# The first stage of a fused attention, gating and mixing kernel in another order

## The chip, the cores and the metric

The kernel runs on one core of a Trainium2 chip. The core has a matrix engine (PE), a vector engine (DVE), an engine for activations and copies (ACT), a general engine (POOL), and a queue engine (SP) from which nearly all DMA transfers of this kernel are issued. Each engine runs its own instructions in order, and waits for the others through semaphores. The metric is the device time of one execution in microseconds (us); lower is better.

## The reference, cut to what matters

```python
# attention in chunks of 64 (8 batches, 8 heads, 576 tokens, head width 64)
scores = scale * np.matmul(q_c, k_c.transpose(0, 1, 2, 4, 3))
attn = softmax(scores); x = np.matmul(attn, v_c)          # -> (8, 576, 512)
# gated MLP
h = np.maximum(x @ w_in, 0.0)                             # w_in 512 x 1024
u, v = h[..., :512], h[..., 512:]
v_n = (v - mu) / np.sqrt(var + 1e-06)
v_s = np.einsum('ts,bsd->btd', w_spatial, v_n) + b_spatial[None, :, None]
x = (u * v_s) @ w_out
# token and channel mixer
u = x + (np.maximum(x.T @ w_tok1, 0.0) @ w_tok2).T
out = u + np.maximum(u @ w_ch1, 0.0) @ w_ch2
```

q, k and v are float32. The weights of the gated MLP and of the mixer are float64 and are brought to float32 on the core.

## The kernel before, in words

The program has two halves. In the first, attention and gated MLP run batch by batch, and attention of batch b+1 is woven into the gated MLP of batch b; in the second, the mixer runs over all batches. Matrix products are made in three passes of a high and a low part of each operand (PASSES, line 20). The order of the work is written by hand as three strings of words: FIRST (lines 24 to 36) for batch 0, the conversion of the weights and the attention of batch 1; STEADY for each of the batches 1 to 6; LAST for batch 7 and the way into the second half. `play` (line 1168) calls the function of each word in turn, each engine gets its instructions in that order, and nothing is moved afterwards. So a word early in the string stands early in the queue of every engine that it uses, and a word that waits holds all later words of its engine.

What the words of FIRST stand for (a digit behind a word is a head pair 0 to 3 with 4 for the last 64 tokens, a token block, a column block or a weight piece):

- Attention, with the prefix a for batch 0 and none for batch 1: l, v or L load (SP); in batch 0 x turns q and k on PE and y copies them out (L355, and L349 for the last tokens, ACT); in batch 1 x is transposed on DVE (L377, L378). S scores (PE, L391, L400), s maximum and subtraction (DVE, L410, L411), e exponential (ACT, L417), n row sum and reciprocal (DVE, L421 to L423), z scaling (POOL, L427), T transposes of the probabilities (PE, L435), t their copy (ACT, L443), P times v (PE, L459, L467), p and q high and low part of the result (ACT L478, L488; DVE L480, L492). In batch 1 x4, S4 and so on belong to the last tokens or, for loads and x, to the first pairs of batch 2 (L4, L5, x4).
- Weight pieces 0 to 11: 0 to 3 are the v half of w_in, 4 to 7 its u half by columns, 8 to 11 w_out by columns. wl loads (SP, L130), wa first step (ACT, L144, L145), wm middle (DVE, L153, L155), we end (POOL, L163), wi high part (ACT, L185), wj and wk low part (DVE or POOL, L188).
- Token weights: gl loads them (SP), gt turns one block of columns (PE, L246), gh splits it: a copy on ACT (L83) and a low part on DVE (L84), for the last block, gh4, two copies L256, two small ones L262 and L263 on ACT, and L257 and L264 on DVE.
- Gated MLP: Y is a quarter of the v product of token blocks 0 to 3 (PE, L536), V2 that of the last block (L565); R relu (ACT, L583), r statistics (DVE, L588, L589), F and G add the last block's halves (ACT, L574, L575; DVE, L579), rs and rq give the reciprocal deviation (DVE, L593, L595; ACT, L598, with a load of the activation table), N normalizes (DVE, L602), i and Q high and low part (ACT, L608; DVE, L617), U u product (PE, L625), E relu of it (ACT, L635), W token product (PE, L648), M gate (DVE, L658), H and J its parts (ACT, L661; DVE, L664), A, B and O output product (PE, L674), D its copy and store (ACT, L681; SP, L682).

Several words share storage, and so wait for each other. The products Y, V, U, W, A and O take turns in two buffers of the accumulator memory (`ps_mm`, line 97, two tiles); a new one waits until the one two before has been read. The transposed token weights and P share one bank (tag "p", lines 242 and 449), so a gt waits for p and q of the P before it, and a P waits for the gh before it. Weight pieces 4 to 11 are loaded into two buffers (tag "craw", line 127); attention's q and k take four buffers (tag "raw", line 293), v three (tag "vt", line 359).

Of the kernel before, what the change touches and what calls it, by code (L numbers as in the profile page):

```python
# [10 lines left out]
U32 = mybir.dt.uint32  # L11
# [12 lines left out]
FIRST = """  # L24
al0 wl0 al1 wl1 Z9 ax0 ay0 wa0 aS0 as0 ax1 al2 av0 wl2 wm0 ae0 ay1 an0 we0 az0 aS1 as1 wa1 aT0 wi0 wm1
at0 ax2 al3 av1 wl3 we1 wk0 ae1 ay2 an1 az1 aP0 aS2 ap0 as2 wi1 aq0 aT1 wa2 ae2 at1 ax3 av2 wm2 ay3 an2
az2 aP1 av3 aS3 as3 ap1 ae3 aq1 wj1 ax4 ay4 aT2 we2 wa3 wi2 at2 an3 wm3 az3 gl0 gl1 gl2 wl4 wl5 aP2 aS4
as4 ap2 wk2 we3 aq2 Y0 ae4 aT3 at3 wi3 an4 wk3 az4 Y1 aP3 L0 ap3 aq3 wa4 aT4 at4 Y2 aP4 wm4 ap4 aq4 Y3
x0 we4 wl6 wa5 L1 gt0 wi4 R0 R1 gh0 wm5 r0 S0 V2 s0 wk4 R3 we5 gt1 wi5 F r1 e0 R2 r3 wa6 G r2 gh1 wk5
U0 wl7 n0 x1 R4 z0 wm6 gt2 r4 we6 rs rq gh2 wi6 S1 U1 E0 wk6 s1 N0 T0 gt3 wa7 i0 Q0 t0 e1 gh3 N1 U2  # L30
wm7 n1 N2 we7 gt4 i1 wi7 E1 z1 Q1 gh4 wk7 i2 N3 N4 L2 wl8 U3 i4 Q2 x2 P0 p0 L3 S2 i3 E2 Q3 T1 q0 Q4
W0 t1 E3 s2 wl9 wa8 wm8 wa9 W1 we8 x3 e2 M0 M1 wi8
wm9 S3 W2 n2 wl10 we9 H0 wa10 W3 M2 s3 H2 wi9 J0 wl11 M3 z2 P1 S4 wk8 H1 J1 wj9 p1 q1 J2 H3
e3 wm10 T2 J3 A0 s4 n3 we10 A1 wa11 t2 L4 z3 wi10 B0 wm11 D0 e4 B1 P2 p2 D1 we11 T3 wj10 O2 n4
q2 t3 x4 z4 L5 P3 T4 wi11 p3 q3 D2 wk11 t4 O3 P4 D3 p4 q4
"""
STEADY = """
x1 ca L2 S0 V0 s0 e0 ca n0 z0 cm ce V1 cm S1 R1 r1 R0 r0 ce T0 R2 r2 R3 r3 t0 V2 U0 s1 e1
# [17 lines left out]
def attention_gmlp_mixer(  # L56
# [17 lines left out]
    DM = 512  # L74
# [1108 lines left out]
    pieces = by_rows(w_in, w_in_t, DM) + by_cols(w_in, w_in_t) + by_cols(w_out, w_out_t)  # L1183

    def load_piece(i):
        if i < 4:

            if i % 2 == 0:
                pieces[i].raw = pieces[i + 1].raw = lp.tile(
                    [128, 2, DM, 2], U32, tag=f"g{i // 2}", bufs=1, name="wv_raw")  # L1190
            pieces[i].load(pieces[i].raw[:, i % 2])
        else:
            pieces[i].load()

    class Stream:
# [19 lines left out]
    play(FIRST, {  # L1215
        **attn[0].ops("a"), **attn[1].ops(), **Gate(0).ops(), "Z": warm,
        "wl": load_piece, "wa": lambda i: pieces[i].start(), "wm": lambda i: pieces[i].mid(),
        "we": lambda i: pieces[i].end(), "wi": lambda i: pieces[i].to_hi(),
        "wj": lambda i: pieces[i].to_lo(nc.vector), "wk": lambda i: pieces[i].to_lo(nc.gpsimd),
# [34 lines left out]
    c1, s1 = {}, {}  # L1254
# [70 lines left out]
    for b in range(NB):  # L1325
        for n in range(21):
            g, i = divmod(n, 7)
# [9 lines left out]
    for n in range(7 * NB):  # L1337
        b, i = divmod(n, 7)
# [53 lines left out]
```

## Time and profile before

| what | value |
|---|---|
| timed runs, median (3 runs) | 1242.53 us (1241.91 to 1242.74) |
| the profiled execution | 1244.85 us |
| its span, first to last instruction | 1242.3 us |
| PE busy | 1192.9 us, 96% of the span |
| weight loads of PE busy | 1127.6 us, 91% |
| DVE busy | 879.5 us, 71% |
| ACT busy | 501.0 us, 40% |
| POOL busy | 161.7 us, 13% |
| mean granted PE clock | 0.984 of full |
| DMA, mean over the span | 158 GB/s |

A row of the timeline gives the start in us from the span's start, the time that it takes, the engine, the line of the kernel, the operation, output and input tiles, shapes and count; in brackets the idle time of the engine before it and the engine and line that ended it. A row of the waits gives who waited for whom, the total in us, how often, and the longest. A row of the windows gives a stretch, its length, the busy time of each engine with its count of instructions, the granted clock of PE, the share of the DMA engines and GB/s. Times of a group of equal instructions run from the first start to the last end. Busy shares say little here, because the program has stages with different limits; the first stage, up to about 118 us, is what the change touches.

### The profile page before, as it was taken

The numbers are of one execution on the slowest core, as the hardware profiler recorded it, in microseconds if no ns is written. First come the engines' busy times: TensorE is split into PE (matmuls) and PEld (weight loads), VectorE is DVE, ScalarE is ACT, GpSimd is POOL, SyncE is SP. The second block draws the span as 40 slices with busy tenths as digits, with TensorE's granted clock in tenths as the row PEclk, the third lists the DMA queues.
The fourth block names the chain that finished last, engine by engine and source line by source line (L and its number), as shares of the span: only waits on it lengthen the run. The fifth ranks groups of instructions, "written<-read, shape, count | busy, mean of one in ns | idle before, by whom it ended". The sixth has DMA issues, their size and how long they took to land. (4 is left out here: it accounts for less than half of the span.)

```text
span 1242.3 us, 25079 instructions
## 1 busy us (share of the span) xinstructions
PE 1192.9 (96%) x10042; PEld 1127.6 (91%) x10042; DVE 879.5 (71%) x1365; ACT 501.0 (40%) x797; POOL 161.7 (13%) x156
## 2 busy tenths in 40 slices
PE   6889999999999999998899999999998999999997
PEld 5779898989898989997889999999998999999997
DVE  5667757576766767366776776776768887787786
ACT  5464535354545444434332232332225434334431
POOL 2323111111121121013400000000005100000000
PEclk8889999999999999999989999999999999999999
DMA  9735537484838381178445565565385576666773
GB/s 228 150 77 127 96 104 134 100 172 107 200 85 206 89 213 38 56 158 203 140 142 170 170 189 172 163 187 166 134 303 190 195 217 199 183 188 189 214 213 45
DMA packets 405704, 196.00 MB, mean 158 GB/s; under 512 B 348434, under 2 KB 368338, under 8 KB 405588
## 3 DMA queue, kind: packets, MB, share of 16 engines
q1 hardware_dynamic: 400724, 193.81, 58.9%
q8 instruction: 79, 1.29, 0.5%
q10 hardware_dynamic: 4864, 0.59, 0.3%
q14 instruction: 37, 0.30, 0.1%
HBM read 123.16 MB, written 71.17 MB: 156 GB/s over the span
## 5 line engine op out<-in xcount | busy, mean ns | idle before, releaser
L1010 PE MATMUL ps_c<-ub,wt 128*128 128x288 f32 x2016 | 288.9, 298 | 6.6 <-ACT s L1042 2.5
L1010 PEld LDWEIGHTS ps_c<-ub,wt 128*128 128x128 f32 x2016 | 278.2, 190 | 12.9 <-ACT s L1042 3.8
L1010 PE MATMUL ps_c<-hb,wt 128*128 128x288 f32 x2016 | 268.9, 295 | 1.6 <-DVE hb L1099 1.6
L1010 PEld LDWEIGHTS ps_c<-hb,wt 128*128 128x128 f32 x2016 | 268.2, 188 | 2.2 <-DVE hb L1099 2.2
L625 PE MATMUL ps_u<-xt,w_in 128*128 128x288 f32 x768 | 110.3, 304 | 7.7 <-ACT ut L635 3.3
L625 PEld LDWEIGHTS ps_u<-xt,w_in 128*128 128x128 f32 x768 | 107.3, 195 | 9.1 <-ACT ut L635 3.5
L1098 ACT CAST hb<-h 128x1728 fp32r<-128x1728 f32 x40 | 64.8, 1638 | 122.7 <-DVE h L1091 50.0
L648 PE MATMUL ps_s<-ws,vn 128*128 128x288 f32 x768 | 108.5, 297 | 2.8 <-ACT ut L635 2.8
L648 PEld LDWEIGHTS ps_s<-ws,vn 128*128 128x128 f32 x768 | 103.5, 188 | 4.7 <-ACT ut L635 4.4
L674 PE MATMUL ps_o<-g,w_out 128*128 128x288 f32 x768 | 106.6, 296 | 0.0
L674 PEld LDWEIGHTS ps_o<-g,w_out 128*128 128x128 f32 x768 | 102.5, 188 | 1.0 <-ACT h L899 0.2
L1099 DVE TENSOR_TENSOR hb<-h,hb 128x1728 fp32r<-128x1728 f32 x40 | 78.2, 1955 | 28.6 <-ACT hb L1098 28.6
L536 PE MATMUL ps_v<-w_in,xt 128*128 128x512 f32 x384 | 92.7, 399 | 0.0
L536 PEld LDWEIGHTS ps_v<-w_in,xt 128*128 128x128 f32 x384 | 72.1, 190 | 16.7
L427 POOL TENSOR_TENSOR e<-e,sm 128x512 f32<-128x512 f32 (+1 forms) x40 | 39.1, 976 | 236.6 <-DVE sm L423 194.3
L163 POOL TENSOR_TENSOR ctmp<-ctmp,craw 128x512 uint32<-128x512 uint32 (+3 forms) x41 | 49.6, 1211 | 135.4 <-DVE ctmp L155 64.6
L926 PE MATMUL ps_u<-w,h 128*128 128x288 f32 x384 | 62.2, 299 | 4.4 <-DVE xh L931 4.4
L967 ACT CAST ub<-xh 128x576 fp32r<-128x576 f32 x56 | 37.4, 672 | 70.0 <-DVE xh L974 66.8
L926 PEld LDWEIGHTS ps_u<-w,h 128*128 128x128 f32 x384 | 54.8, 190 | 5.7 <-DVE xh L931 5.5
L968 DVE TENSOR_TENSOR ub<-xh,ub 128x576 fp32r<-128x576 f32 x56 | 43.0, 770 | 21.1 <-ACT ub L967 20.6
L868 ACT CAST xn<-nat 128x512 fp32r<-128x512 f32 x40 | 24.8, 619 | 76.8 <-DVE nat L866 75.6
L887 PE MATMUL ps_h<-xn,w 128*128 128x512 f32 x192 | 51.8, 403 | 3.4 <-ACT xn L868 3.3
(148 smaller groups left out, 1609.5 us busy)
## 6 DMA issues: line engine op xcount, KB each, us to landing
hd<-c SPq DMA_DIRECT2D x120, 288.0 KB, 2.2
h<-hd SPq DMA_DIRECT2D x40, 864.0 KB, 6.9
craw<-in_moe_w_ch_dram SPq DMA_DIRECT2D x24, 512.0 KB, 4.9
x_raw<-x2d SPq DMA_DIRECT2D x160, 64.0 KB, 2.7
xh<-x2d SPq DMA_DIRECT2D x16, 576.0 KB, 6.0
u2d<-xh SPq DMA_DIRECT2D x16, 576.0 KB, 3.1
u<-u2d SPq DMA_DIRECT2D x16, 576.0 KB, 6.8
x2d<-x2o SPq DMA_DIRECT2D x31, 288.0 KB, 2.9
```

The lines of the kernel that those rows point to most:

```text
L163: nc.gpsimd.tensor_tensor(out=tu, in0=tu, in1=raw[:, :, 0], op=ALU.add)
L427: nc.gpsimd.tensor_tensor(out=e, in0=e, in1=sm.to_broadcast([128, e.shape[1], 64]), op=ALU.mult)
L536: nc.tensor.matmul(ps, lhsT=self.xt[kc][:, p, 128 * ti:128 * ti + 128], rhs=w_in_t[r][:, kc, DM:2 * DM], start=kc == 0 and n == 0, stop=kc ...
L625: nc.tensor.matmul(ps[:, h, 0:HALF], lhsT=w_in_t[r][:, kc, 128 * m:128 * m + 128], rhs=self.xt[kc][:, p, HALF * h:HALF * h + HALF], start= ...
L648: nc.tensor.matmul(ps[:, h, 0:HALF], lhsT=lhsT, rhs=rhs[:, HALF * h:HALF * h + HALF], start=n == 0, stop=n == len(ops) - 1)
L674: nc.tensor.matmul(ps[:, h, 0:HALF], lhsT=w_out_t[r][:, kc, 128 * m:128 * m + 128], rhs=self.g[p][:, kc, h], start=kc == 0 and n == 0, sto ...
L887: nc.tensor.matmul(ps[kk], lhsT=PB["w1"][r][:, m, ksl], rhs=xn[:, p], start=m == 0 and n == 0, stop=False)
L926: nc.tensor.matmul(ps, lhsT=h1[:, kk, p, 128 * m:128 * m + 128], rhs=PB["w2"][r][:, kk, HALF * h:HALF * h + HALF], start=n == 0, stop=n == 5)
L968: eng.tensor_tensor(out=lo, in0=x, in1=f32(hi), op=ALU.subtract)
L1010: nc.tensor.matmul(ps, lhsT=lhsT, rhs=rhs, start=first and n == 0, stop=n == len(ops) - 1, skip_group_check=True)
L1098: nc.scalar.copy(out=hi, in_=x)
L1099: nc.vector.tensor_tensor(out=lo, in0=x, in1=f32(hi), op=ALU.subtract)
```

## The change

Only FIRST and the loading of two weight pieces change. The string's first two lines and half of its third stay; the rest is written in another order:

```diff
-az2 aP1 av3 aS3 as3 ap1 ae3 aq1 wj1 ax4 ay4 aT2 we2 wa3 wi2 at2 an3 wm3 az3 gl0 gl1 gl2 wl4 wl5 aP2 aS4
...
+az2 aP1 av3 aS3 as3 ap1 aq1 wj1 ae3 aT2 at2 ax4 ay4 we2 an3 wa3 wi2 az3 wm3 gl0 gl1 gl2 wl4 wl5 wl6 wl7
...
     def load_piece(i):
-        if i < 4:
+        if i < 4 or 6 <= i < 8:
 
             if i % 2 == 0:
                 pieces[i].raw = pieces[i + 1].raw = lp.tile(
-                    [128, 2, DM, 2], U32, tag=f"g{i // 2}", bufs=1, name="wv_raw")
+                    [128, 2, DM, 2], U32, tag=f"g{i // 2 % 3}", bufs=1, name="wv_raw")
             pieces[i].load(pieces[i].raw[:, i % 2])
```

Pieces 6 and 7, the second half of w_in's u half, are loaded into the buffer that held pieces 0 and 1 (tag "g0"), not into the two buffers of pieces 4 and 5, and stand on SP's queue directly behind these, ahead of the attention loads L0 and L1 of batch 1. The token weights are turned between the head pairs of batch 0 and the Y products: gt0 ahead of Y0, gt1 behind Y1, gt2 behind Y3, gt3 behind U0, gt4 behind U1, and P0 of batch 1 directly behind gt4. The four relus R0, R1, R3, R2 follow each other. The string has one line less, so that each later line has a number lower by one than in the kernel before; the rows below carry each kernel's own numbers.

The first place is ACT behind the exponential of head pair 3 of batch 0. `last` are the copies y of the last tokens, `wv_raw` and `w_in` belong to weight pieces 3 and 2, and `aT` is the copy at2. Before:

```order
L417 ACTIVATE e<-e 128x512
L349 COPY last_167<-ps_x 128x256
L349 COPY last_168<-ps_x 128x256
L144 ACTIVATE ctmp<-wv_raw 128x512
L145 ACTIVATE wv_raw<-wv_raw 128x512
L185 CAST w_in_84<-ctmp 128x512
L443 COPY aT<-ps_t 128x512
```

and after the change:

```order
L416 ACTIVATE e<-e 128x512
L442 COPY aT<-ps_t 128x512
L348 COPY last_167<-ps_x 128x256
L348 COPY last_168<-ps_x 128x256
L143 ACTIVATE ctmp<-wv_raw 128x512
L144 ACTIVATE wv_raw<-wv_raw 128x512
L184 CAST w_in_84<-ctmp 128x512
```

The copy at2 has moved ahead of five instructions.

The second place is ACT from the exponential e1 of batch 1 to the high part of weight piece 7 (the last `w_in` row in both). `ws_r` are the parts of gh4, `vn` and `vr` high parts i of the normalized v, `ut` the relus E. Before:

```order
L417 ACTIVATE e<-e 128x512
L83 CAST ws_88<-ps_w 128x576
L608 CAST vn_92<-v_163 128x512
L185 CAST w_in_84<-ctmp 128x4x128
L635 ACTIVATE ut<-ps_u 128x576
L256 CAST ws_r_90<-ps_w 64x576 x2
L262 CAST ws_r_91<-ws_rows 1x576
L263 CAST ws_r_91<-ws_rows 1x576
L608 CAST vn_92<-v_164 128x512
```

and after the change, in two pieces, up to gh4 and from there to piece 7:

```order
L416 ACTIVATE e<-e 128x512
L184 CAST w_in_84<-ctmp 128x4x128
L634 ACTIVATE ut<-ps_u 128x576
L143 ACTIVATE ctmp<-wv_raw 128x512
L144 ACTIVATE wv_raw<-wv_raw 128x512
L607 CAST vn_92<-v_164 128x512
L255 CAST ws_r_90<-ps_w 64x576 x2
```

and from gh4's one-row copies on to piece 7:

```order
L261 CAST ws_r_91<-ws_rows 1x576
L262 CAST ws_r_91<-ws_rows 1x576
L607 CAST vn_92<-v_165 128x512
L477 CAST xt<-ps_p 128x512
L634 ACTIVATE ut<-ps_u 128x576
L607 CAST vr_94<-v_166 128x512
L609 CAST vr_95<-v_166 64x512
L184 CAST w_in_84<-ctmp 128x4x128
```

Before, piece 7's high part stood ahead of gh4; now it stands seven rows behind it, and piece 6's (the first `w_in` row) and both first steps of piece 7 stand between e1 and gh4.

The third place is ACT at the end of the stage, around the high part of the last weight piece (the last `w_out` row), the parts p4 (`xt`, four copies) and the output copies D (`x2o`). Before:

```order
L443 COPY aT<-ps_t 128x512
L185 CAST w_out_86<-ctmp 128x4x128
L478 CAST xt<-ps_p 128x512
L681 COPY x2o<-ps_o 128x576
L443 COPY aT<-ps_t 128x256
L681 COPY x2o<-ps_o 128x576
L488 CAST xt<-ps_p 128x64 x4
```

and after the change:

```order
L680 COPY x2o<-ps_o 128x576 x2
L442 COPY aT<-ps_t 128x256
L487 CAST xt<-ps_p 128x64 x4
L184 CAST w_out_86<-ctmp 128x4x128
L680 COPY x2o<-ps_o 128x576 x2
```

The last weight piece's high part now stands behind p4, no longer ahead of p3.

More of the change, by code (lines that the diff above doesn't have):

```diff
@@ L26 @@
 at0 ax2 al3 av1 wl3 we1 wk0 ae1 ay2 an1 az1 aP0 aS2 ap0 as2 wi1 aq0 aT1 wa2 ae2 at1 ax3 av2 wm2 ay3 an2
-az2 aP1 av3 aS3 as3 ap1 ae3 aq1 wj1 ax4 ay4 aT2 we2 wa3 wi2 at2 an3 wm3 az3 gl0 gl1 gl2 wl4 wl5 aP2 aS4
[L28 to L35, printed above, removed]
+az2 aP1 av3 aS3 as3 ap1 aq1 wj1 ae3 aT2 at2 ax4 ay4 we2 an3 wa3 wi2 az3 wm3 gl0 gl1 gl2 wl4 wl5 wl6 wl7
+aP2 aS4 as4 ap2 aq2 wk2 ae4 aT3 at3 we3 an4 wi3 gt0 wk3 az4 Y0 gh0 wa4 L0 aP3 ap3 aq3 wm4 Y1 gt1 we4 wa5
+aT4 at4 gh1 wm5 wi4 Y2 x0 aP4 ap4 aq4 we5 wk4 L1 Y3 gt2 R0 R1 R3 R2 r0 wi5 S0 gh2 r1 V2 F r2 r3 s0 wk5
+G R4 e0 U0 r4 rs rq x1 n0 z0 wa6 gt3 N0 gh3 i0 E0 wm6 S1 T0 t0 U1 Q0 N1 we6 i1 s1 gt4 e1 wi6 E1 Q1 N2 wa7
+i2 gh4 wk6 P0 n1 wm7 L2 wl8 U2 Q2 N3 i3 z1 we7 p0 E2 N4 i4 wi7 Q3 q0 x2 wk7 T1 t1 U3 S2 Q4 s2 E3 W0 P1
+e2 p1 q1 L3 wl9 n2 wa8 wm8 z2 W1 we8 x3 M0 wi8 wa9 wm9 T2 t2 S3 W2 s3 M1 H0 wl10 we9 e3 n3 J0 z3 P2 p2
+W3 M2 H1 wi9 wa10 q2 J1 wk8 S4 wl11 H2 M3 wm10 T3 t3 s4 J2 H3 e4 we10 wj9 J3 A0 P3 p3 n4 wa11 A1 wi10 q3
+L4 z4 B0 wm11 D0 B1 D1 T4 t4 we11 wj10 O2 P4 p4 wi11 q4 D2 wk11 x4 L5 O3 D3
 """
```

## The prediction, on record before the changed kernel was run

> **What bounds the kernel now.** I read the page first, then the core's windows cut where the first stage changes character, then what the matrix engine (PE) waited for between 28 and 119 us, then the granted clock in slices of one microsecond, then the timeline row by row.
>
> ```profile
> span 1242.3 us, 25079 instructions
> ```
> ```profile
> 0.00:28.10 28.10, 19.04 (x253) 15.93 (x253) 15.06 (x27) 13.66 (x24) 8.38 (x13) 0.88 0.98 213
> 28.10:47.70 19.60, 16.05 (x152) 12.89 (x153) 10.28 (x25) 10.27 (x24) 8.33 (x8) 0.91 0.65 171
> 47.70:85.20 37.50, 28.53 (x266) 25.29 (x264) 26.74 (x53) 21.95 (x38) 10.90 (x9) 0.82 0.59 97
> 85.20:118.40 33.20, 33.20 (x378) 31.96 (x380) 25.18 (x47) 16.54 (x31) 11.10 (x9) 1.00 0.53 117
> ```
> ```profile
> PE ps_p L459 <- ACT aT L443: 3.6, 1, 3.6
> PE ps_u L625 <- ACT ut L635: 3.3, 1, 3.3
> PE ps_u L625 <- ACT v L583: 3.2, 1, 3.2
> PE ps_u L625 <- POOL w_in L188: 1.2, 1, 1.2
> ```
> ```profile
> 56.00:57.00 1.00, 1.00 (x6) 0.50 1.43 148
> ```
>
> The windows give length, then busy time of PE, its weight loads, DVE, ACT and POOL, the clock, and the DMA. From 85.2 to 118.4 us PE is never idle; from 28.1 to 85.2 it is idle for 12.5 us, and 11.3 of those are the four waits shown. The last row shows a second price: a microsecond after the idle stretch of 3.18 us that ended at 55.25 the clock is 0.50. So 28 to 85 us is where a new order can gain; behind it PE is full, and there a new order can only lose. The steady batches and the second half of the program keep their order, so I forecast the start of the second batch's first score matmuls (118.42 now), and carry its shift to the end.
>
> **The change part by part.** All line numbers are those of before. First the head of the stage, where the copy of the third pair's probabilities goes ahead of weight piece 3.
>
> ```profile
> 31.00 0.59 ACT L443 COPY aT<-ps_t 128x512 f32<-128x512 f32 x1
> 31.65 1.06 PE L459 MATMUL ps_p<-aT,vt 64*64 64x64 f32 x32 [3.56 <-ACT aT L443]
> 33.46 3.85 PE L536 MATMUL ps_v<-w_in,xt 128*128 128x512 f32 x12
> 34.44 0.68 DVE L480 TENSOR_TENSOR xt<-ps_p,xt 128x512 fp32r<-128x512 f32 x1
> 44.63 3.05 PE L536 MATMUL ps_v<-w_in,xt 128*128 128x512 f32 x12
> 34.72 2.56 SPq L297 DMA_DIRECT2D qk_raw<-in_k_dram  x4
> 60.06 0.80 PE L246 MATMUL ps_w<-ident,ws_rows 128*128 128x128 f32 x5
> ```
>
> The copy now follows the exponential directly, so aP2 starts near 29.5 instead of 31.65: 2.1 us gained. But the first token-weight transpose, gt0, now stands ahead of Y0 on PE, and it needs the bank that aq2 (the DVE row at 34.44) frees. Moved 2.1 us up, aq2 would end at 33.0; behind the DVE work already queued there I put 33.8. With gt0's 0.80, Y0 starts at 34.65, 1.2 later than now. Y0 to Y3 with P3, gt1, T4 and P4 between them need 14.1 us (four times 3.05, gt1's 0.80, and 1.1 that I put for the other three), so Y3 ends at 48.7, against 47.68. The gain at aP2 has become two transposes done early.
>
> Pieces 6 and 7 load ahead of L0 (their buffers held pieces 0 and 1, long converted). One more megabyte, at the 213 GB/s of the first window, holds L0 back by 4.9 us: its key issues end at 42.2 instead of 37.28 and land, at some 3 us each, about 45; x0 is reached at 45.3, and S0, which needs it, at 49.5. I cost that at nothing, with 2 to 3 us of cover.
>
> Then the middle. These rows price each step; where two starts follow on one engine, I take their distance.
>
> ```profile
> 46.82 1.11 ACT L583 ACTIVATE v<-ps_v 128x512 f32<-128x512 f32 x2
> 47.02 1.28 POOL L188 TENSOR_TENSOR w_in<-ctmp,w_in 128x512 fp32r<-128x512 f32 x1 [2.00 <-ACT w_in L185]
> 53.69 0.66 DVE L588 BATCH_NORM_STATS2 st<-v 128x6 f32<-128x512 f32 x1
> 54.49 0.67 DVE L579 TENSOR_TENSOR v<-ps_v,v_sum 128x512 f32<-128x512 f32 x1
> 57.55 0.68 DVE L421 TENSOR_REDUCE sm<-e 128x8 f32<-128x512 f32 x1
> 58.64 0.71 DVE L377 STREAM_TRANSPOSE qkT<-qk_raw 128x512 f32<-128x512 f32 x1
> 58.84 1.04 POOL L427 TENSOR_TENSOR e<-e,sm 128x512 f32<-128x512 f32 x1 [4.63 <-DMA qk_raw<-in_k_dram]
> 60.12 0.38 DVE L153 TENSOR_SCALAR ctmp<-ctmp 128x512 uint32<-128x512 uint32 x1
> 61.15 0.69 DVE L588 BATCH_NORM_STATS2 st<-v 128x6 f32<-128x512 f32 x1
> 61.87 3.46 PE L625 MATMUL ps_u<-xt,w_in 128*128 128x288 f32 x24
> 62.73 0.19 DVE L595 RECIPROCAL rs<-rs 128x5 f32<-128x5 f32 x1
> 64.40 0.68 DVE L410 TENSOR_REDUCE mx<-ps_s 128x8 f32<-128x512 f32 x1
> 65.79 0.54 DVE L602 TENSOR_SCALAR v<-v,mv,rs 128x512 f32<-128x512 f32 x1
> 67.48 1.28 ACT L417 ACT_TABLE_LOAD   x1
> 73.68 0.62 ACT L185 CAST w_in<-ctmp 128x512 fp32r<-128x512 f32 x1 [1.86 <-POOL ctmp L163]
> 74.75 1.26 ACT L256 CAST ws_r<-ps_w 64x576 fp32r<-64x576 f32 x2
> 76.05 0.75 DVE L257 TENSOR_TENSOR ws_r<-ps_w,ws_r 64x576 fp32r<-64x576 f32 x1 [0.27 <-ACT ws_r L256]
> 76.72 0.67 ACT L263 CAST ws_r<-ws_rows 1x576 fp32r<-1x576 f32 x1
> 76.95 5.65 PE L625 MATMUL ps_u<-xt,w_in 128*128 128x288 f32 x22 [1.20 <-POOL w_in L188]
> 85.20 3.46 PE L648 MATMUL ps_s<-ws,vn 128*128 128x288 f32 x24 [0.27 <-ACT ut L635]
> ```
>
> Prices: an ACT copy 0.55 behind another; a bn pair 0.8 (53.69 to 54.49); a score's softmax start 1.39 (64.40 to 65.79); a row sum with reciprocal 1.09 (57.55 to 58.64); the transposes x 1.48; a weight mid step 1.03; 24 u-matmuls 3.46; a POOL step on a weight piece 1.28; the low part of a token-weight turn as L257, 0.75. P and T groups I put at 0.65, S at the 1.1 of the row in the next fence.
>
> With the four relus together, U0's slot is free by 50.0; gt2, S0 and V2 (eight matmuls of Y's form, 8/12 of 3.05) are ahead of U0 until 52.5. The 3.2 us wait is gone, and U0 with gt3 is done at 56.7. What is late next is S1. ACT runs R3, R2, wi5 and gh2 after Y3 (2.3 us, to 51.0), and DVE, in order, has gh2's low part ahead of r1: 51.8. Then r1, r2, r3 (2.4), s0 (1.4), G (0.7), R4 on ACT (0.6), r4 and the rstd rows (61.15 to 62.92, 1.8): 58.7. x1 ends at 60.2. **PE waits 3.5 us for S1**, and after S1's 1.1 another 1.1 for T0 (n0 1.1, z0 on POOL 1.0: 62.4). U1 and gt4 end at 67.2.
>
> DVE goes on from 61.3: N0, gh3, wm6, Q0, N1, 3.4 us, 64.7. ACT waits for that N1 and then has, before gt4's results are copied: i1, table load 1.28, e1, wi6, E1, two for wa7, i2, together 5.3: 70.0. The two L256 copies end at 71.3, L257 at 72.05, and only then is the bank of P0 free. **PE waits 4.9 us for P0**, which now stands ahead of U2. DVE is held too: L264 waits for ACT's last two copies (0.67 each) and is over at 73.4, with n1, wm7 and all the later normalizing queued behind. n1 and wm7 end at 75.5, we7 on POOL (behind z1) at 76.9. wi7 stands on ACT behind i3, p0, E2 and two of i4, which start when DVE reaches N3 at 76.7: 2.75, then 0.62, then wk7 1.28: 81.4. U2 and T1 are over at 76.8, U3 issues two matmuls and **waits 4.3 us for wk7**. Its other 22 need 3.2 at full clock, S2 1.1: W0 starts at 85.7, against 85.20. The whole middle is a wash, +0.5.
>
> Third, the tail, where PE had no wait to lose.
>
> ```profile
> 118.42 1.10 PE L391 MATMUL ps_s<-qkT,qkT 64*64 64x64 f32 x32
> 118.83 0.57 ACT L488 CAST xt<-ps_p 128x64 fp32r<-128x64 f32 x4
> 131.53 0.69 DVE L588 BATCH_NORM_STATS2 st<-v 128x6 f32<-128x512 f32 x1 [3.86 <-ACT v L583]
> ```
>
> wi11, the high part of the last weight piece, now stands on ACT behind p4, and so waits for P4; O3 follows P4 on PE and needs wi11 and wk11. From P4's end: p4's copies 0.57, wi11 0.62, wk11 1.28, 2.47 together, less the two matmuls that need only wi11 (0.27): 2.2 lost. Of S3, whose transposes x3 on DVE stand behind q1 (so behind P1), I reckon 5.0 us from P1's end against W1 and T2 with 4.4: 0.6 lost. A0 misses 0.2 for the third low gate. L5 is issued behind D2's store, about 5 us later; that delays x1 and s0 of the steady loop on DVE, which sits idle for 3.9 us there (the row at 131.53) and must deliver T0's input only 13 us after the first score: nothing, if that cover holds, and 1 to 2 us if not.
>
> Sum: 0.5 + 0.6 + 0.2 + 2.2 = +3.5 us at full clock. The clock was not in it. In before the 22 matmuls at 76.95 took 5.65, where 22/24 of 3.46 is 3.17: 2.5 lost to half clock. The three waits of the new order are as long as those that halved it, but a slow U1 or U2 hides in the next wait; only U3 pays directly, and Y0, if the thin stretch from 28.5 to 34.6 counts as idle. So the clock adds from nothing to 1.7 for Y0 and 2.5 for U3; I take 0.5. Forecast: +4.0.
>
> [...]
>
> The profiled execution took 1244.85 us, its span 1242.3 with 2.55 around it; the median of the timed runs is 1242.53, so I add the shift to the median: 1246.5. One measurement of this kernel can tell about 0.2% (2.5 us) from no change.
>
> **The rivals.** Faster: DVE's total work, not the waits between engines, sets W0. The stage holds 26.7 us of it (third window), which from r0 at 48 would run to 75. If ACT reaches gt4's copies by 67.2, when DVE gets to L257, then n1 and wm7 run at once, wk7 is done by 74.5 and W0 starts at 79: 6.2 sooner, less the 3.0 of the tail, -3.2, 1239.3. The point that decides is whether gt4's copies come before 68. For it: DVE is only 71% busy there now (26.74 of 37.50). Against it: ACT is in order and has eight rows of its own between N1 and those copies. Chance 0.12.
>
> No change that can be measured: Y3 ends as early as now (1.2 gained) and the tail loses only what O3 loses, with the clock full throughout: +0.5 to +2.5, about 1244. For it: my 33.8 for aq2 is the softest number. Chance 0.28.
>
> Slower than I forecast: half clock in Y0 and in U3, 1.7 + 2.5 on top of 3.5, and L5 uncovered: +8, 1250.5. Part of the slower cases, chance 0.15 of their 0.60; the forecast itself has 0.45.
>
> That the loads of pieces 6 and 7 come no sooner can be excluded: nothing still in use holds their buffers, and they stand directly behind pieces 4 and 5 on the queue.
>
> **How the numbers follow.** Forecast 1246.5. The low end is 1.5 us under the median, half way to the faster rival, which leaves most of that rival out; the high end is the slowest case: 1241 to 1250.5. Faster 0.12, same 0.28, slower 0.60 (0.45 and 0.15).
>
> **What would show it.** In the new profile PE's waits should name x1 (DVE L377) or its successor for S1 with about 3.5, DVE L257 for P0 with 4 to 5, POOL L188 for U3 with about 4 and again for O3 with about 1 after one on ACT L185; the wait of 3.6 at aP2 should be cut to about 1. W0 should start between 85 and 89, S2 just before it. The forecast is wrong if W0 starts before 82, or if O3 runs without a gap.

## The result and the profile after

The changed kernel takes 1256.51 us (median; 1255.91 to 1256.97) against 1242.63 us before: ratio 1.0104, 95% interval 1.0091 to 1.0118. It is slower by 13 to 14 us; the forecast was slower by 4.0. The sign was right, the size wrong by more than a factor of three, and the range up to 1250.5 did not hold it. The profiled execution took 1256.38 us, its span 1254.4.

The windows of the changed kernel, cut at the end of Y3 (51.1), at W0 (91.6) and at the next batch's first scores S0 (131.8); columns as before: length, busy time of PE, its weight loads, DVE, ACT and POOL, granted clock, DMA.

```profile
span 1254.4 us, 25087 instructions
```
```profile
0.00:28.10 28.10, 18.59 (x244) 15.68 (x244) 14.61 (x27) 13.65 (x24) 7.96 (x13) 0.88 0.95 208
28.10:51.10 23.00, 19.79 (x174) 15.03 (x173) 14.23 (x30) 11.84 (x26) 10.77 (x9) 0.85 0.92 217
51.10:91.60 40.50, 28.65 (x256) 26.25 (x254) 26.70 (x50) 21.43 (x36) 9.28 (x7) 0.79 0.34 72
91.60:131.80 40.20, 36.24 (x384) 34.05 (x380) 25.56 (x50) 16.15 (x32) 10.98 (x9) 0.96 0.37 84
```

Y3 ends 3.5 us later than before, W0 starts 6.4 later (91.64 against 85.20), S0 13.4 later (131.79 against 118.42). After S0 nothing is lost: the span grew by 12.1. The last stretch, in which PE was never idle before, now has 4 us of idle time and a clock of 0.96. PE's waits between 28 and 132 us:

```profile
PE ps_p L458 <- DVE ws_r L256: 3.7, 1, 3.7
PE ps_s L390 <- DVE last L377: 3.3, 1, 3.3
PE ps_t L434 <- POOL e L426: 3.1, 3, 1.3
PE ps_u L624 <- ACT w_in L184: 2.8, 1, 2.8
PE ps_s L390 <- DVE qkT L376: 1.3, 1, 1.3
PE ps_o L673 <- ACT w_out L184: 1.2, 1, 1.2
...
PE ps_w L245 <- PE ps_t L434: 0.9, 1, 0.9
PE ps_o L673 <- POOL w_out L187: 0.8, 1, 0.8
PE ps_u L624 <- POOL w_in L187: 0.8, 1, 0.8
...
```

All the waits that the forecast named are there: P0 behind DVE L256, S1 behind x1, U3 behind piece 7, O3 behind ACT and then POOL; the wait of 3.6 at aP2 is cut to 1.0, and U0's is gone. W0, expected between 85 and 89, came at 91.64. Two waits that are not in that list are T3's for POOL and gt0's, about a microsecond each. The view puts gt0's down to T3, but T3 ended at 33.50; gt0 starts at 34.43, 0.10 us behind the DVE row of aq2, which frees its bank, as the prediction had it (gt0 starts 0.10 us behind aq2 in a_w7, a_gh2 and a_p0 too):

```profile
33.65 0.68 DVE L479 TENSOR_TENSOR xt<-ps_p,xt 128x512 fp32r<-128x512 f32 x1
```

The rows of PE's timeline on which the lost time lies (start, length, and in brackets the idle time ahead and what ended it):

```profile
29.89 0.69 PE L458 MATMUL ps_p<-aT,vt 64*64 64x64 f32 x32 [1.01 <-ACT aT L442]
...
32.38 1.12 PE L434 MATMUL ps_t<-ident,e 128*128 128x128 f32 x4 [1.26 <-POOL e L426]
34.43 1.38 PE L245 MATMUL ps_w<-ident,ws_rows 128*128 128x128 f32 x5 [0.94 <-PE ps_t L434]
35.75 4.61 PE L535 MATMUL ps_v<-w_in,xt 128*128 128x512 f32 x12
...
65.14 5.56 PE L624 MATMUL ps_u<-xt,w_in 128*128 128x288 f32 x24
...
85.94 4.69 PE L624 MATMUL ps_u<-xt,w_in 128*128 128x288 f32 x22 [0.82 <-POOL w_in L187]
...
115.52 0.53 PE L673 MATMUL ps_o<-g,w_out 128*128 128x288 f32 x2 [0.65 <-DMA vt<-in_v_dram]
...
127.15 4.71 PE L673 MATMUL ps_o<-g,w_out 128*128 128x288 f32 x22 [0.82 <-POOL w_out L187]
```

Y0 takes 4.61 us, where twelve matmuls of this form take 3.05 at full clock and Y0 itself took 3.85 before; U1, U3 and O3 are stretched in the same way (U3 took 5.65 before). The row at 115.52 names a DMA long done; it was the gate's low part on DVE, which ends at 115.46 (in a_fill the same wait of 0.65 us is put down to that DVE row). One-microsecond slices within two of the long rows (U1 and O3) give the reason, the last three numbers of a row being clock, DMA share and GB/s:

```profile
66.00:67.00 1.00, 1.00 (x6) 1.00 (x6) 1.00 (x1) 0.12 (x1) 1.00 (x1) 0.50 0.55 88
...
129.00:130.00 1.00, 1.00 (x6) 1.00 (x5) 0.00 (x0) 0.00 (x0) 0.00 (x0) 0.50 0.80 129
```

In such slices from 28 us to S0, idle time sums to 12.5 us before and 19.0 after, and busy time times the missing part of the clock to 6.7 and 11.6. Of the 13.4 us, then, 6.5 are idle time, 4.9 half clock, and 2.0 slightly longer rows and a start later by 0.4.

### The profile page after: what moved, and what is told of

Its sections match the earlier page's. It is cut to its first block, busy times and chain, and to the rows that moved or that the text cites. A ratio compares the mean times of both kernels' runs of the same rounds, so it can differ in the third digit from the quotient of the medians.

```text
span 1254.4 us, 25087 instructions
## 1 busy us (share of the span) xinstructions
PE 1198.1 (96%) x10042; PEld 1131.7 (90%) x10042; DVE 881.4 (70%) x1365; ACT 501.0 (40%) x797; POOL 161.9 (13%) x156
## 5 line engine op out<-in xcount | busy, mean ns | idle before, releaser
L162 POOL TENSOR_TENSOR ctmp<-ctmp,craw 128x512 uint32<-128x512 uint32 (+3 forms) x39 | 46.6, 1194 | 113.6 <-DVE ctmp L154 66.0
```

What stands on the lines that cost most here:

```text
L162: nc.gpsimd.tensor_tensor(out=tu, in0=tu, in1=raw[:, :, 0], op=ALU.add)
```

## The experiments

The marks in this section are counted from the start of aP1, the second pair's products, because what is ahead of it waits for loads and lies at 22.5 to 25.1 us from one profiled execution to the next. Each ratio is to the kernel before, timed on the same chip.

| kernel | ratio (95%) | W0 | S0 | S0 against its base |
|---|---|---|---|---|
| before | 1 | 60.55 | 93.77 | |
| after | 1.0104 (1.0091 to 1.0118) | 66.59 | 106.74 | +12.97 |
| a_tail | 1.0088 (1.0074 to 1.0101) | 66.79 | 103.06 | -3.68 |
| a_gt0 | 1.0116 (1.0099 to 1.0133) | 66.80 | 106.95 | +0.21 |
| a_w7 | 1.0070 (1.0056 to 1.0083) | 60.05 | 100.06 | -6.68 |
| a_fill | 1.0101 (1.0087 to 1.0115) | 64.69 | 103.29 | -3.45 |
| a_gh2 | 1.0100 (1.0081 to 1.0118) | 66.22 | 106.39 | -0.35 |
| a_head | 1.0073 (1.0061 to 1.0085) | 63.62 | 103.78 | -2.96 |
| a_all | 0.9996 (0.9988 to 1.0005) | 57.19 | 93.53 | -13.21 |
| a_p0 | 1.0099 (1.0085 to 1.0113) | 66.84 | 106.99 | +0.25 |
| a_x1 | 1.0097 (1.0082 to 1.0113) | 66.84 | 107.02 | +0.28 |
| b_copy | 0.9968 (0.9956 to 0.9981) | 56.79 | 90.02 | -3.75 |
| b_relu | 1.0013 (1.0001 to 1.0025) | 60.83 | 94.06 | +0.29 |
| b_load | 1.0008 (0.9997 to 1.0018) | 61.06 | 94.46 | +0.69 |
| b_fill2 | 0.9941 (0.9930 to 0.9953) | 54.50 | 87.91 | -5.86 |
| b_w7 | 0.9926 (0.9914 to 0.9938) | 52.48 | 85.71 | -8.06 |
| b_best | 0.9938 (0.9924 to 0.9951) | 53.13 | 87.25 | -6.52 |

The base is the changed kernel for names with a, the kernel before for names with b. The marks are of one profiled execution each, and such executions differ: Y0, behind the same wait of about 3.56 us at aP2, took 3.85 us in the kernel before, 3.69 in b_relu and 5.10 in b_load. The ratio, times 1242 us, agrees with S0's distance from that of the kernel before within 1.7 us, but for a_w7 (2.4) and a_fill (3.0), whose timed runs gained less than their profiled ones.

**The end of the stage (a_tail).**

```diff
- we11 wj10 O2 P4 p4 wi11 q4 D2 wk11 x4 L5 O3 D3
+ we11 wi11 wj10 O2 wk11 P4 p4 L5 q4 x4 D2 O3 D3
```

> The changed kernel with one thing undone at the end of the stage: the high part of the last weight piece and its low part stand ahead of p4, and L5 ahead of D2's store, as before the change. Theory (the tail pays by itself for the last weight piece: 1.19 and 0.82 us of waits in O3, and 1.5 us of half clock in the 22 matmuls behind them): 3.5 us less than the changed kernel, about 1253.0 us, with O3 free of waits and at full clock. Rival (the next stage's start is held by its own loads, so that a sooner O3 only makes S0 wait): no change, 1256.5 us.

O3 and S0 on PE:

```profile
121.88 0.46 PE L466 MATMUL ps_p<-aT,vlast 64*64 64x64 f32 x16
122.27 3.44 PE L673 MATMUL ps_o<-g,w_out 128*128 128x288 f32 x24
125.65 1.15 PE L390 MATMUL ps_s<-qkT,qkT 64*64 64x64 f32 x32
```

O3 runs as one row of 3.44 us with no wait, and S0 comes 3.7 us sooner. The theory held: 2.0 us of waits and 1.5 us of half clock behind them. The timed runs show it less sharply: by the ratios it is 2 us, and the intervals of a_tail and of the changed kernel overlap.

**The head (a_gt0, a_head).** First gt0 alone behind Y0; then T3 and gt0 both, with Y1 ahead of P3:

```diff
- ae4 aT3 at3 we3 an4 wi3 gt0 wk3 az4 Y0 gh0 wa4 L0 aP3
+ ae4 aT3 at3 we3 an4 wi3 wk3 az4 Y0 gt0 gh0 wa4 L0 aP3
```

> The changed kernel with the first token-weight transpose gt0 behind Y0 instead of ahead of it. Theory (gt0 waits for the bank and holds Y0 by some 2 us, and all later steps hang on Y3): Y0 starts about 2 us sooner, W0 too, 1254.5 us. Rival (the middle is set by the queues of DVE and ACT, which have cover there): the sooner Y0 is lost in a longer wait for S1, 1256.5 us.

```diff
- ae4 aT3 at3 we3 an4 wi3 gt0 wk3 az4 Y0 gh0 wa4 L0 aP3 ap3 aq3 wm4 Y1 gt1
+ ae4 Y0 aT3 at3 we3 an4 wi3 gt0 wk3 az4 gh0 wa4 L0 Y1 aP3 ap3 aq3 wm4 gt1
```

> The changed kernel with Y0 directly behind the third pair's products, as before the change: the transposes T3 and gt0 stand behind Y0, and Y1 ahead of P3. Theory (the 2.1 us gained at aP2 were given back because PE idles for 2.2 us at T3 and gt0 and then runs Y0 at half clock): Y0 starts 1.2 us behind aP2 instead of 5.9, at full clock, Y3 ends about 4 us sooner, and W0 comes 3 us sooner: 1252 us. Rival (the loads of L0, late behind two more pieces, hold x0 and S0; or DVE's and ACT's queues have that time as cover): W0 at most 1 us sooner, 1254.5 us.

PE's rows of a_gt0, from T3 to P3, and of a_head, from aP2 to T3:

```profile
30.16 1.12 PE L434 MATMUL ps_t<-ident,e 128*128 128x128 f32 x4 [1.24 <-POOL e L426]
30.93 4.11 PE L535 MATMUL ps_v<-w_in,xt 128*128 128x512 f32 x12
...
37.20 0.69 PE L458 MATMUL ps_p<-aT,vt 64*64 64x64 f32 x32 [1.52 <-DVE ws L83]
```
```profile
27.79 0.69 PE L458 MATMUL ps_p<-aT,vt 64*64 64x64 f32 x32 [1.43 <-ACT aT L442]
...
28.95 3.05 PE L535 MATMUL ps_v<-w_in,xt 128*128 128x512 f32 x12
31.84 0.60 PE L434 MATMUL ps_t<-ident,e 128*128 128x128 f32 x4
```

With gt0 alone moved, Y0 does start 2.6 us closer to aP2, but T3's wait remains, Y0 still runs partly at half clock (4.11), and P3 now waits 1.5 us for the bank of gt0; Y3 ends 0.7 us sooner and W0 not at all. With T3 behind Y0 too, Y0 follows aP2 by 1.2 us at full clock, Y3 ends 2.8 us sooner, W0 3.0 sooner. So the head's loss is carried to W0 in full. gt0's bank did hold Y0, but moving gt0 alone, as my theory for a_gt0 had it, is no cure; what a_head adds is T3, which needs the fourth pair's probabilities from POOL, and Y1 as cover for gt0's bank. No run moves T3 alone. The late loads of L0, a_head's rival, held nothing.

**Piece 7 (a_w7).** Its first steps go ahead of E1, its middle step ahead of gh4's low part, its high part directly behind gh4:

```diff
- e1 wi6 E1 Q1 N2 wa7 i2 gh4 wk6 P0 n1 wm7 L2 wl8 U2 Q2 N3 i3 z1 we7 p0 E2 N4 i4 wi7 Q3 q0 x2 wk7 T1
+ e1 wi6 wa7 E1 Q1 N2 wm7 wk6 we7 i2 gh4 P0 n1 wi7 L2 wl8 U2 Q2 N3 i3 wk7 z1 p0 E2 N4 i4 Q3 q0 x2 T1
```

> The changed kernel with the steps of weight piece 7 sooner: its first ACT steps ahead of E1, its middle step on DVE ahead of gh4's low part, its high part on ACT directly behind gh4. Theory (the chain gh4, n1, wm7, we7, wi7, wk7 sets U3, and so W0): U3 starts behind T1 with no wait, 3 to 5 us sooner, and at full clock: 1251 to 1252 us. Rival (DVE's queue of normalized v, q0 and x2 is the limit, and W0 or S2 waits in place of U3): at most 1 us less, 1255.5 us or more.

PE, from P0 to W0:

```profile
72.10 1.13 PE L458 MATMUL ps_p<-aT,vt 64*64 64x64 f32 x32 [3.44 <-DVE ws_r L256]
73.16 5.33 PE L624 MATMUL ps_u<-xt,w_in 128*128 128x288 f32 x24
78.34 0.60 PE L434 MATMUL ps_t<-ident,e 128*128 128x128 f32 x4
78.69 3.43 PE L624 MATMUL ps_u<-xt,w_in 128*128 128x288 f32 x24
...
83.13 3.45 PE L647 MATMUL ps_s<-ws,vn 128*128 128x288 f32 x24
```

U3 follows T1 without a wait and at full clock, and W0 starts 6.5 us sooner though P0 still waits 3.44. DVE's normalizing, the rival, was no limit. This one chain is worth as much as the whole of W0's delay against before. The profiled execution was the fastest of the five timed ones; by the ratios the gain is 4.2 us, clear of noise but less than the 6.7 of the marks.

**The waits for S1 and P0 (a_gh2, a_x1, a_p0).** Three moves at the two longest waits: gh2 behind s0; x1 ahead of the rows that need R4; P0 behind U2.

```diff
- wi5 S0 gh2 r1 V2 F r2 r3 s0 wk5
+ wi5 S0 r1 V2 F r2 r3 s0 gh2 wk5
...
- G R4 e0 U0 r4 rs rq x1 n0 z0
+ x1 G R4 e0 U0 r4 rs rq n0 z0
...
- gh4 wk6 P0 n1 wm7 L2 wl8 U2 Q2
+ gh4 wk6 n1 wm7 L2 wl8 U2 P0 Q2
```

> The changed kernel with gh2 (ACT's copy and DVE's low part of the third token-weight turn) behind the v statistics r1 to r3 and the softmax start s0, and behind the copies F, instead of ahead of r1. Theory (DVE, in order, is held by gh2's low part, so that x1 and S1 come late): DVE starts r1 some 2 to 2.7 us sooner, the wait of 3.3 us for S1 falls to about 1 us, and W0 comes 2 to 2.7 us sooner, 1252.3 us. Rival (x1 is set by R4 and the copies F, which hang on V2): the wait for S1 stays over 2.5 us and the time does not change, 1255 us.

> The changed kernel with the transposes x1 on DVE ahead of G, r4 and the rstd rows, so that S1 no longer stands behind R4. Theory (S1's wait is set by x1's place behind the rows that need R4; S1 and its softmax start feed e1, the gh4 copies and piece 7's chain): S1's wait falls from 3.3 to about 1 us, and W0 comes 1 to 2 us sooner, 1253.5 us. Rival (N0 and N1 come later by the 1.6 us of x1, and i1, which ACT runs ahead of e1, with them): S1's wait goes, W0 does not move, 1255 us.

> The changed kernel with P0 of batch 1 behind U2 instead of ahead of it; only PE's order changes. Theory (piece 7's chain gh4, n1, wm7, we7, wi7, wk7 sets U3, so that P0's wait of 3.7 us is paid by time that U3 waits anyway): U2 starts some 4 us sooner, U3's wait grows by as much, W0 stays within 1 us: 1255 us. Rival (P0's wait is on the path): W0 3 to 4 us sooner, 1251.5 us.

a_gh2 left S1's wait at 3.0 us and W0 within 0.4: my theory fell, its rival held. S1 stood behind x1's place after R4, as a_x1 shows by taking the wait away; but there T0 then waits instead. PE's rows of a_x1 (S1, T0), and of a_p0 (P0, T1, U3):

```profile
58.98 1.15 PE L390 MATMUL ps_s<-qkT,qkT 64*64 64x64 f32 x32 [0.56 <-DVE last L377]
63.95 1.12 PE L434 MATMUL ps_t<-ident,e 128*128 128x128 f32 x4 [3.81 <-POOL e L426]
```
```profile
74.25 0.69 PE L458 MATMUL ps_p<-aT,vt 64*64 64x64 f32 x32
77.98 0.66 PE L434 MATMUL ps_t<-ident,e 128*128 128x128 f32 x4 [3.03 <-POOL e L426]
83.77 0.85 PE L624 MATMUL ps_u<-xt,w_in 128*128 128x288 f32 x2 [5.14 <-ACT w_in L184]
```

In a_p0 the 3.7 us that U2 no longer waits come back as waits for T1 and U3. In both W0 is 0.3 us later than in the changed kernel, less than its own timed runs differ by (1.06 us). The two longest waits of the changed kernel cost nothing of their own.

**The clock (a_fill).** PE gets work whose results are not used, at five waits:

```diff
+            for _ in range(n):
+                nc.tensor.matmul(ps, lhsT=w_in_t[0][:, 0, DM:DM + 128],
+                                 rhs=w_in_t[0][:, 0, DM:2 * DM], start=True, stop=True)
...
- aP2 aS4 as4 ap2
+ aP2 aS4 ZM5 as4 ap2
...
- wm6 S1 T0
+ wm6 ZT11 S1 T0
...
- wk6 P0 n1
+ wk6 ZT12 P0 n1
...
- t1 U3 S2
+ t1 ZS10 U3 S2
...
- x4 L5 O3
+ x4 ZS5 L5 O3
```

ZM, ZT and ZS issue n of these matmuls into a PSUM bank that is free there (of the Y and U products, of the transposes T, of the scores).

> The changed kernel with idle matmuls (results not used) put into five of PE's waits: 5 ahead of T3, 11 ahead of S1, 12 ahead of P0, 10 ahead of U3, 5 ahead of O3, each for less time than the wait lasts. They take no wait away and only keep PE busy. Theory (the clock was the term that I made too small: half clock costs 1.5 us in Y0, 1.5 in U3 and 1.5 in O3, while a slow U1 and U2 hide in the waits behind them): 4 to 4.5 us less, about 1252.3 us, with a granted clock of 1.00 through the stage. Rival (the half clock only fills time that the waits would take anyway): 1256 us; or more, if the fillers delay what stands behind them.

The clock's share of the lost time falls from 11.6 to 4.5 us, Y0 takes 3.04, O3's 22 matmuls 3.17, and S0 comes 3.45 us sooner. U3 kept its half clock (5.29): with a faster U2 its fillers ended 2.7 us before piece 7 was there. The four timed runs, however, spread over 1252.46 to 1255.89 us, the profiled one lowest, and their ratio does not differ from the changed kernel's. In this kernel the clock's price is thus shown in the trace only.

**All of it (a_all).** The edits of a_head, a_w7 and a_tail, and x3 ahead of piece 8's middle step:

```diff
- L3 wl9 n2 wa8 wm8 z2 W1 we8 x3 M0
+ L3 wl9 n2 wa8 x3 wm8 z2 W1 we8 M0
```

> The changed kernel with four things mended at once: the head as in the run with Y0 ahead of T3, piece 7's steps sooner, the last piece's steps and L5 ahead of p4 and D2, and in the tail x3 ahead of piece 8's middle step. Theory (what the change lost lies in these places and adds up: 3 us in the head, 6.5 at U3, 3.7 at O3, 1.3 at S3): 1240 to 1243 us, as fast as the kernel before or a little faster. Rival (they share their cover, so that each wait removed grows another): half of the sum, 1248 us.

The ratio is 0.9996: in sum the loss is gone. By the marks the three edits gave 3.0, 6.7 and 3.7 us alone, 13.3 together, and all at once 13.2, so they add up and x3 added nothing: S3 no longer waits, but W2 and W3 then wait 1.1 us for DVE's gates. (By the ratios they gave 3.9, 4.2 and 2.0 us, 10.1 together, and all at once 13.4.) Not every part is mended: W0 now comes 3.4 us sooner than in the kernel before, but from W0 to S0 it still takes 36.3 us instead of 33.2. That rest no run explains.

**The parts alone, on the kernel before (b_copy, b_relu, b_load).**

```diff
- ap1 ae3 aq1 wj1 ax4 ay4 aT2 we2 wa3 wi2 at2 an3 wm3 az3
+ ap1 aq1 wj1 ae3 aT2 at2 ax4 ay4 we2 an3 wa3 wi2 az3 wm3
...
- wi4 R0 R1 gh0 wm5 r0 S0 V2 s0 wk4 R3 we5 gt1 wi5 F r1 e0 R2 r3
+ wi4 R0 R1 R3 R2 gh0 wm5 r0 S0 V2 s0 wk4 we5 gt1 wi5 F r1 e0 r3
...
- wl4 wl5 aP2 ... we4 wl6 wa5 ... U0 wl7 n0
+ wl4 wl5 wl6 wl7 aP2 ... we4 wa5 ... U0 n0
```

> The kernel before with one part of the change: the exponential ae3, the transposes aT2 and the copy at2 ahead of the turn x4, its copies y4 and weight piece 3; all else as before. Theory (the 2.1 us gained at aP2 are real but end in the wait for U0, which hangs on DVE's and ACT's queues): Y0 to Y3 come about 2 us sooner, W0 at most 1 us sooner, 1241 us. Rival (the gain is carried through): 2 us less, 1239.5 us; and against both, if the idle time in the head halves the clock elsewhere, no change.

> The kernel before with one part of the change: the relus R3 and R2 directly behind R0 and R1 on ACT, ahead of gh0. Theory (U0's wait of 3.2 us goes, but U3 and W0 hang on later queues): U0 starts about 3 us sooner and at full clock, and W0 comes at most 1 us sooner, 1241 us. Rival (U0's wait is on the path): W0 some 3 us sooner, 1238.5 us.

> The kernel before with one part of the change: weight pieces 6 and 7 loaded into the buffer of pieces 0 and 1, directly behind pieces 4 and 5, ahead of L0 and L1. Theory (transfers are hidden on both sides): no change, 1241.6 us within 1 us. Rival (L0 comes 4.9 us later and x0, and so S0, waits for it): S0 of batch 1 up to 2 us later, 1243.5 us.

The third part does not show the edit of `load_piece`, which is that of the change. The copies alone are a clear gain of 4 us, twice what the more generous of the two expectations allowed. PE in b_copy, aP2 to Y0:

```profile
27.80 0.69 PE L459 MATMUL ps_p<-aT,vt 64*64 64x64 f32 x32 [1.02 <-ACT aT L443]
...
28.96 3.05 PE L536 MATMUL ps_v<-w_in,xt 128*128 128x512 f32 x12
```

The wait falls from 3.56 to 1.02, and with it the half clock that the kernel before had in Y0 (3.85 there); all of it reaches W0. The relus together remove U0's wait, but W0 stays, as the theory had it: gt2 then waits 2.2 us and S1 1.6, and U1 runs at half clock (5.13). The sooner loads change nothing that can be told: W0 comes 0.5 us later, behind a Y0 of 5.10 us.

**Further from b_copy (b_fill2, b_w7, b_best).** To the kernel of b_copy come fillers ahead of U0 (ZT10) and U3 (ZT14); or piece 7's steps sooner, as in the diff; or both, with ZT10 ahead of U0 and ZT3 ahead of gt4 and U3.

```diff
- Q0 t0 e1 gh3 N1 U2 wm7 n1 N2 we7 gt4 i1 wi7 E1 z1 Q1 gh4 wk7 i2
+ Q0 wm7 we7 t0 e1 gh3 wi7 N1 U2 n1 N2 gt4 i1 E1 wk7 z1 Q1 gh4 i2
```

> The kernel before with the copies ahead of weight piece 3, and idle matmuls (results not used) in two of PE's waits: 10 ahead of U0 and 14 ahead of U3. They take no wait away. Theory (half clock costs 1.5 us in U0, which hides in the wait for the fifth token-weight turn, and 2.4 us in U3, which does not): U3's 22 matmuls take 3.2 us instead of 5.6, 1236.3 us. Rival (the throttle does not follow such short idle stretches, or the fillers delay what is behind them): 1238.7 us or more.

> The kernel before with the copies ahead of weight piece 3 (the part that was 4 us faster alone), and with piece 7's middle step on DVE ahead of gh3's low part and its high part on ACT ahead of i1, so that E1 no longer stands behind it. Theory (E1, in ACT's order behind piece 7, and then wk7 hold U3 by 4.5 us and halve its clock): both waits go, U3 runs at full clock, W0 comes 3 to 5 us sooner, 1234 to 1236 us. Rival (the normalized v on DVE is next): 1238.5 us.

> The fastest kernel so far (the kernel before with the copies ahead of piece 3 and piece 7's steps sooner) with idle matmuls (results not used) ahead of U0 (10), gt4 (3) and U3 (3). Theory (two half-clock spells are left in it, 1.5 us in U0 and 1.5 in U3, and the second is paid in full): 1231.5 to 1232.5 us, with a granted clock of 1.00 from 28 us on. Rival (E1 and the normalized v on DVE already set W0): 1233.3 us.

PE in b_fill2 (U3) and in b_w7 (gt4, U3):

```profile
71.41 0.53 PE L625 MATMUL ps_u<-xt,w_in 128*128 128x288 f32 x2
73.45 3.18 PE L625 MATMUL ps_u<-xt,w_in 128*128 128x288 f32 x22 [1.51 <-POOL w_in L188]
```
```profile
65.47 0.80 PE L246 MATMUL ps_w<-ident,ws_rows 128*64 128x128 f32 x5 [0.98 <-DVE ws L84]
67.13 4.97 PE L625 MATMUL ps_u<-xt,w_in 128*128 128x288 f32 x24 [0.85 <-ACT ut L635]
```

Idle work alone, with no wait removed, brings W0 2.3 us sooner than in b_copy, and the ratios of the two do not overlap: here the clock's price is shown in the timed runs as well. b_w7 is the fastest kernel of the study by its ratio, 1233.34 us against 1242.88 for the kernel before on that chip; its gain was expected, the half clock that U3 kept (4.97) was not. Fillers on top of it bring nothing: U3 takes 3.46 us, but S2 then waits 2.4 us for x2 on DVE, W0's first row is slow in its place (4.33), and W0 is 0.6 us later. That rival held.

## Why the prediction was wrong, point by point

Of the 13.4 us at S0, 4.0 were forecast. The 9.4 that were missing are 2.4 in the head, 3.5 in the middle and 3.9 in the tail, less the 0.5 that I had put for the clock.

- **The head, "two transposes done early".** aP2 did come 2.2 us sooner (counted from aP1). The step that failed is the start of Y0, put at 34.65: it was 35.75. gt0 waited for its bank, as I had said, but aq2 freed it at 34.33, not 33.8, and gt0 then took 1.3 us instead of 0.80, because the clock had fallen to 0.50 at 32.4 us. Ahead of that fall PE had waited 1.01 us at aP2 and 1.26 at T3, which the change puts ahead of gt0 and which needs POOL; T3's wait I had not looked for. Y0 lost another 1.56 us to the half clock. Y3 ended at 51.14 instead of 48.7. a_head shows that this is worth 3.0 us at W0.
- **The middle, "a wash, +0.5".** The waits were near their forecast: S1 3.28 (3.5), T0 1.21 (1.1), P0 3.74 (4.9), U3 3.6 (4.3). That only piece 7's chain sets W0, as in my sum, held too: a_x1 and a_p0 show that S1's and P0's waits cost nothing, a_w7 that this chain costs all. But the chain ended at 85.89, not 81.4. 2.4 us of that came from Y3; the other 2 lie on the way. 0.3 is ACT's wait for the slow U1, ahead of E1; the rest fits DVE rows priced at their shortest, though no run tests it: a step of 0.5 took 1.52, one of 0.69 took 1.42, two of 0.5 took 1.98, each while POOL was running (rows in the last section). Then U3 ran at half clock, 1.5 more. W0 came at 91.64, not 85.7.
- **DVE held by gh2's low part** was wrong as a reason: without it S1 still waited 3.0 us (a_gh2).
- **The tail, "+3.0".** O3's 2.2 was 2.01, by the rows that I named, and undoing that order took these waits away (a_tail). S3's 0.6 was 1.30. What I left out is 1.5 us of half clock behind O3's wait, 0.65 for the third gate (I had 0.2), and 1.5 us of W and O rows a little longer and more often broken, which no run explains. L5 and L0 were hidden, as I said.
- **The clock, "I take 0.5".** This is the most mis-sized term: by the granted clock, 4.9 us more was lost to half clock than before. I wrote that Y0 and U3 could cost 1.7 and 2.5, and then took a value near the lower end; they cost 1.6 and 1.5, and O3, which I had not counted, 1.5, gt0 0.5. No run shows the 1.7, which was my estimate: Y0's twelve matmuls took 4.61 us here, 3.85 in the kernel before and 3.05 at full clock. That a slow U1 and U2 hide in the waits behind them was right but for the 0.3 us of ACT.
- **The rivals.** The slower rival named the right mechanism (half clock in Y0 and U3) and stopped at +8; its other half, L5 uncovered, did not come. The faster one, DVE's total work, hung on gt4's copies before 68: they came at 72.94. That this work sets W0 is excluded by a_w7: its DVE does the same work and W0 comes 6.5 us sooner. That the copies ahead of piece 3 gain something was seen, but not how much: alone they are worth 4 us (b_copy), since Y0's half clock goes with the wait; the places of T3 and gt0, of piece 7 and of the last piece lost 13.3, three and a half times that.

## What to carry to other kernels

Where PE waits several times in a row, price only the chain that ends last, and follow it from its first instruction through every engine's queue: here the two longest waits were free and the next cost 6.7 us by the marks. Where waits come close together, price the half clock that may follow in the work behind them: here 0.50 behind waits of 1.01 and 1.26 us cost Y0 1.56 us. Check a named releaser against the end of its row: here T3 was named for a wait that aq2 ended. Test the parts of a reordering one by one: this one, 13 us slower as a whole, held a part that alone gains 4.

## What the runs showed of the hardware

**The clock fell to 0.50 behind waits of about a microsecond that came close together.** In the changed kernel it fell at 32.4 us, behind waits of 1.01 and 1.26 us, and stayed there until 39.2, with a third wait of 0.94 in between; in b_w7 it was 0.50 from 67.6 to 71.0 us, behind waits of 0.98 and 0.85. Single waits with work on both sides did not do it: 1.30 us ahead of S3 in the changed kernel, 1.43 ahead of aP2 in a_head. Waits of 0.65 and 1.02 us ahead of T2 and aP2 did it in a_fill (0.50 in the slices from 30 to 32 us) but not in b_copy (1.00 there), and 3.18 us ahead of U0 did it in the kernel before (0.50, U0 4.98 us) but not in b_load (1.00, U0 3.45). So how long and how close together is enough is not shown, nor what sets the length of a spell: the first two lasted 6.8 and 3.4 us.

**DVE rows beside POOL rows.** DVE and then POOL in the changed kernel:

```profile
65.85 1.52 DVE L601 TENSOR_SCALAR v<-v,mv,rs 128x512 f32<-128x512 f32 x1
...
69.28 0.54 DVE L601 TENSOR_SCALAR v<-v,mv,rs 128x512 f32<-128x512 f32 x1
...
77.85 1.42 DVE L154 SCALAR_TENSOR_TENSOR ctmp<-wv_raw,ctmp 128x512 uint32<-128x512 uint32 x1
...
79.79 1.98 DVE L601 TENSOR_SCALAR v<-v,mv,rs 128x512 f32<-128x512 f32 x2
```
```profile
65.46 1.62 POOL L162 TENSOR_TENSOR ctmp<-ctmp,wv_raw 128x512 uint32<-128x512 uint32 x1 [1.14 <-ACT ut L634]
...
77.67 1.05 POOL L426 TENSOR_TENSOR e<-e,sm 128x512 f32<-128x512 f32 x1 [5.85 <-DVE sm L422]
79.40 1.63 POOL L162 TENSOR_TENSOR ctmp<-ctmp,wv_raw 128x512 uint32<-128x512 uint32 x1 [0.68 <-issue]
```

The same DVE step takes 0.54 us alone and 1.52 beside a POOL row that started first. Not every DVE row is longer there: a transpose at 126.08 us (L376) took 0.70 beside a POOL row from 125.83 to 127.10, and 0.71 at 131.06 with POOL idle. Why some rows take longer there is not shown: no run here moved a POOL step to test it.
